# One-pass input fold, and 5 of 6 instead of 2 of 3 steps that take their mirrored values from the even part

## Chip, cores, metric

One core of a Trainium2 chip. The metric is the device time of one execution in microseconds (us). All profiled runs are fast; the granted clock of the tensor engine is 0.99 to 1.00 of full speed on the mean of every profile. Ratios are the mean time of one kernel's fast runs over the mean of the other's fast runs of the same rounds, so they differ slightly from the ratio of the medians that are quoted beside them.

## The reference

```python
def _attn_ref(x):                        # x: (8, 3008, 256)
    X = np.fft.fft(x, axis=1)
    X = np.fft.fft(X, axis=2)
    return X.real.astype(np.float32)

def _moe_ref(x, w_gate, w_val, w_out):   # x: 24064 x 256, d_ff 1536
    gate = np.maximum(x @ w_gate, 0.0)
    val = x @ w_val
    return (gate * val @ w_out).astype(np.float32)
```

A real part of a two-dimensional Fourier transform, then a gated feed-forward layer.

## The kernel before

The transform is done by matmuls. Because the input is real and only the real part is wanted, the input is first *folded*: rows s and S-s, columns d and D-d are added and subtracted, and half of the tokens are computed together with their *mirrors* (token S-s). There are 288 steps (8 batches x 3 blocks x 12 slices of d_ff). A step computes 512 tokens of 128 hidden units: gate `G` and value `V` for the tokens, and again for their mirrors. With even part `P` and odd part `Q`, the token is `P + Q` and the mirror `P - Q`. The mirror of the gate is made by a matmul that adds -2Q to `G` in PSUM (the memory that matmuls write to). The mirror of the value is made in one of two ways:

- *unsplit* step: a matmul adds -2Q to `V` ("mirrored value matmul"), and VectorE multiplies gate and value of the mirror;
- *split* step: VectorE saves the even part `E` between the two value matmuls (`even`), later computes 2E - V, and GpSimd multiplies.

```python
    ep = ctx.enter_context(tc.tile_pool(name="ep", bufs=4, space=SB))   # rings of gm and E
    ...
    def split(t):
        return NBLK * NF + 8 <= t < len(steps) and t % 3 != 2
    def mirror_gate(t): ...
        nc.tensor.matmul(e["G"][:, cols], lhsT=wm[0][...], rhs=pqt[b, blk][:, 1, cols],
                         start=False, stop=True, skip_group_check=True)
        e["gm"] = ep.tile([128, 512], F32, tag="gm", name="gm")
        nc.scalar.activation(e["gm"][:, cols], e["G"][:, cols], ACTF.Relu)
    def value(t, part): ...              # part 0: V = P;  part 1: V += Q, then h = gs * V on VectorE
    def even(t): ...                     # E = nb * af + V   (VectorE, between part 0 and part 1)
    def mirror_value(t):
        ...
        if split(t):
            nc.vector.scalar_tensor_tensor(e["E"][:, cols], e["E"][:, cols], 2.0, e["V"][:, cols],
                                           op0=ALU.mult, op1=ALU.subtract)
            mirror_h(t, nc.gpsimd, e["E"])          # h = gm * E on GpSimd
        else:
            nc.tensor.matmul(e["V"][:, cols], lhsT=wm[1][...], rhs=pqt[b, blk][:, 1, cols],
                             start=False, stop=True, skip_group_check=True)
            mirror_h(t, nc.vector, e["V"])
    ...
    for t in range(n + NF):              # one step; `extra` holds loads, transforms of the next batch
        if 0 < t <= n: mirror_gate(t - 1)
        if t < n:      gate(t)
        if 0 < t <= n: value(t - 1, 1) if split(t - 1) else mirror_value(t - 1)
        if t < n and not split(t): value(t, 0); value(t, 1)
        for fn in extra.get(t, ()): fn()
        if t >= NF: out_piece(t - NF, 0)
        if split(t): value(t, 0); even(t)
        if t >= NF: out_piece(t - NF, 1)
        if 0 < t <= n and split(t - 1): mirror_value(t - 1)
        ...                              # one operation of a running fold, on GpSimd (two early on)
```

GpSimd's stream is in program order: the operations of the fold for the batch after next stand between its products `h = gm * E`. A fold of a batch has five chunks. (`if`/`else` condensed above; the whole kernel follows.)

Of the kernel before, what the change touches and what calls it, by code (L numbers as in the profile page):

```python
# [11 lines left out]
F32 = mybir.dt.float32  # L12
BF16 = mybir.dt.bfloat16
I32 = mybir.dt.int32
ALU = mybir.AluOpType
ACTF = mybir.ActivationFunctionType
SB = bass.MemoryType.SB
# [9 lines left out]
def free(ap, offset, *dims):  # L27

    part = list(ap.ap[0])
    return bass.AP(ap.tensor, ap.offset + offset, [part] + [list(d) for d in dims])  # L30
# [12 lines left out]
def kernel(ctx: ExitStack, tc, x, w_gate, w_val, w_out, out):  # L43
# [4 lines left out]
    B, S, D = x.shape  # L48
    DF = w_gate.shape[1]
    NA, NB = 94, 32  # L50
    H = D // 2
    NF = DF // 128
    NKA = 12
    NBLK = 3
    J = NB // 2 + 1

    const = ctx.enter_context(tc.tile_pool(name="const", bufs=1, space=SB))
    xp = ctx.enter_context(tc.tile_pool(name="xp", bufs=1, space=SB))
    xcp = ctx.enter_context(tc.tile_pool(name="xcp", bufs=2, space=SB))
    tp = ctx.enter_context(tc.tile_pool(name="tp", bufs=2, space=SB))  # L60
    hp = ctx.enter_context(tc.tile_pool(name="hp", bufs=2 * NF + 1, space=SB))
    psd = ctx.enter_context(tc.tile_pool(name="psd", bufs=1, space=PS))
# [13 lines left out]
    XC = 3  # L76
# [12 lines left out]

    def fold(b, eng):  # L90

        xl, xh, eo = xt[b]
        for lo in range(1, J - 1, XC):
            hi = min(lo + XC, J - 1)
            n = hi - lo
            x1, e1 = xl[0:NA, lo:hi, :], eo[:, lo:hi, :]
            rev = free(xh[0:NA], (NB // 2 - lo) * D, [-D, n], [1, D])
            c1 = xcp.tile([NA, XC, D], F32, tag="xc", name="xc")[:, 0:n, :]
            yield eng.tensor_tensor(c1, x1, rev, op=ALU.subtract)  # L99
            yield eng.tensor_tensor(x1, x1, rev, op=ALU.add)  # L100
            yield eng.tensor_tensor(e1[:, :, H + 1:D], c1[:, :, 1:H], free(c1, D - 1, [D, n], [-1, H - 1]),
                                    op=ALU.subtract)
            eng.tensor_copy(free(e1, 0, [D, n], [H, 2]), free(x1, 0, [D, n], [H, 2]))
            yield eng.tensor_tensor(e1[:, :, 1:H], x1[:, :, 1:H], free(x1, D - 1, [D, n], [-1, H - 1]), op=ALU.add)  # L104
        ends = free(xl[0:NA], 0, [(J - 1) * D, 2], [H, 2])
        eng.tensor_copy(free(eo[:], 0, [(J - 1) * D, 2], [H, 2]), ends)
        for op, o in ((ALU.add, 1), (ALU.subtract, H + 1)):
            yield eng.tensor_tensor(
                free(eo[:], o, [(J - 1) * D, 2], [1, H - 1]), free(xl[0:NA], 1, [(J - 1) * D, 2], [1, H - 1]),
                free(xl[0:NA], D - 1, [(J - 1) * D, 2], [-1, H - 1]), op=op)  # L110
# [158 lines left out]
    with tc.tile_pool(name="sp", bufs=1, space=SB) as sp:  # L269
# [88 lines left out]
        for cs, (o0, d1) in enumerate(((8.0, -8.0), (16.0, -8.0))):  # L358
            o = sp.tile([128, 1], F32, tag=f"off{cs}")
# [13 lines left out]
        for cs in range(2):  # L373
            t2 = sp.tile([128, 4, NB], F32, tag=f"m2t{cs}")
# [27 lines left out]
        for _ in fold(1, nc.gpsimd):  # L402
            pass
# [13 lines left out]
    op = ctx.enter_context(tc.tile_pool(name="op", bufs=2, space=SB))  # L417

    steps = [(b, blk, f) for b in range(B) for blk in range(NBLK) for f in range(NF)]
# [6 lines left out]

    def split(t):

        return NBLK * NF + 8 <= t < len(steps) and t % 3 != 2

    def gate(t):
        b, blk, f = steps[t]
        pq, fs = pqt[b, blk], slice(f * 128, (f + 1) * 128)
        e = ht[t] = {"h": hp.tile([128, 2, 512], BF16, tag="h", name="h"),
                     "G": psg.tile([128, 512], F32, tag="g", name="G"),
                     "gs": gp.tile([128, 512], F32, tag="gs", name="gs")}
        nc.tensor.matmul(e["G"][:], lhsT=wc[0][:, fs], rhs=pq[:, 0, :], start=True, stop=False)  # L437
        nc.tensor.matmul(e["G"][:], lhsT=ws[0][:, fs], rhs=pq[:, 1, :], start=False, stop=True)  # L438
        nc.scalar.activation(e["gs"][:], e["G"][:], ACTF.Relu)  # L439
        cols = mirrored(t)  # L440
        if cols.stop - cols.start < 512:

            lo = 0 if cols.start else cols.stop
            nc.gpsimd.memset(e["h"][:, 1, lo:lo + NB], 0.0)

    def mirror_gate(t):
        b, blk, f = steps[t]
        e, cols = ht[t], mirrored(t)
        nc.tensor.matmul(e["G"][:, cols], lhsT=wm[0][:, f * 128:(f + 1) * 128], rhs=pqt[b, blk][:, 1, cols],  # L449
# [4 lines that stand above are left out]
    def value(t, part):  # L454
        b, blk, f = steps[t]
        e, pq, fs = ht[t], pqt[b, blk], slice(f * 128, (f + 1) * 128)
        if part == 0:
            e["V"] = psv.tile([128, 512], F32, tag="v", name="V")
            nc.tensor.matmul(e["V"][:], lhsT=wc[1][:, fs], rhs=pq[:, 0, :], start=True, stop=split(t))  # L459
        else:  # L460
            nc.tensor.matmul(e["V"][:], lhsT=ws[1][:, fs], rhs=pq[:, 1, :], start=False, stop=True,  # L461
                             skip_group_check=split(t))
            nc.vector.tensor_tensor(e["h"][:, 0, :], e["gs"][:], e["V"][:], op=ALU.mult)  # L463

    def even(t):
        b, blk, f = steps[t]
        e, cols = ht[t], mirrored(t)
        e["E"] = ep.tile([128, 512], F32, tag="e", name="E")
        nc.vector.scalar_tensor_tensor(e["E"][:, cols], nbt[b, blk][:, cols], af[:, f:f + 1], e["V"][:, cols],  # L469
                                       op0=ALU.mult, op1=ALU.add)  # L470
# [8 lines left out]
    def mirror_value(t):  # L479
        b, blk, f = steps[t]  # L480
        e, cols = ht[t], mirrored(t)
# [3 lines that stand above are left out]
            mirror_h(t, nc.gpsimd, e["E"])  # L485
        else:
            nc.tensor.matmul(e["V"][:, cols], lhsT=wm[1][:, f * 128:(f + 1) * 128], rhs=pqt[b, blk][:, 1, cols],  # L487
                             start=False, stop=True, skip_group_check=True)
            mirror_h(t, nc.vector, e["V"])
# [38 lines left out]
    def at(t, fn, *args):  # L528
        extra.setdefault(t, []).append(lambda: fn(*args))

    for k in range(4):
# [3 lines left out]
    at(9, nyquist)  # L535


    plan = {0: (28, 34, (14, 16, 18, 19, 21, 23, 24, 25), 26, 33, (33, 34, 36, 38, 40, 42)),
            1: (12, 19, range(11, 19), 19, 26, (26, 27, 29, 31, 33, 35)),
            2: (7, 13, range(6, 14), 14, 22, (23, 25, 27, 29, 31, 33))}  # L540
    for b in range(B):
        t0 = b * NBLK * NF
        tl, tf, t1, tsh, tr, t2 = plan[min(b, 2)]
        if b + 2 < B:
            at(t0 + tl, load_x, b + 2, nc.sync)
            at(t0 + tf, lambda b=b: folds.append(fold(b + 2, nc.gpsimd)))
        if b + 1 < B:
            for c, k in zip((1, 2, 3, 4, 5, 6, 7, 0), t1):
                at(t0 + k, stage1, b + 1, c, "act")
            at(t0 + tsh, shuffle_out, b + 1, 0, 8)  # L550
            at(t0 + tsh, shuffle_in, b + 1, 0, NKA)
            at(t0 + tr, rotate, b + 1)
            for i, k in enumerate(t2):
                at(t0 + k, stage2, b + 1, i // 2, i % 2, "act")

    folds = []
    n = len(steps)
    for t in range(n + NF):
        if 0 < t <= n:
            mirror_gate(t - 1)  # L560
        if t < n:
            gate(t)
        if 0 < t <= n:
            if split(t - 1):
                value(t - 1, 1)
            else:
                mirror_value(t - 1)
        if t < n and not split(t):
            value(t, 0)
            value(t, 1)  # L570
        for fn in extra.get(t, ()):
            fn()
        if t >= NF:
            out_piece(t - NF, 0)
        if split(t):
            value(t, 0)
            even(t)
        if t >= NF:
            out_piece(t - NF, 1)
        if 0 < t <= n and split(t - 1):  # L580
            mirror_value(t - 1)
        for k in range(2 if t < NBLK * NF + 8 else 1):
            while folds and next(folds[0], folds) is folds:
                folds.pop(0)


# [28 lines left out]
```

## Time and profile before

| | before |
|---|---|
| time, median of 3 (675.66 with the fourth run, used below) | 675.4 us (675.08 to 675.92) |
| PE / VectorE / ScalarE / GpSimd busy | 643.4 / 500.8 / 428.9 / 428.5 us of 673.5 |
| mirrored value matmuls | 126 |
| chain that ended last | PE 94% |

The page of the kernel before, its busy times, slices of GpSimd and PE, and its chain (DVE is VectorE, ACT is ScalarE, POOL is GpSimd):

```profile
PE 643.4 (96%) x4218; PEld 419.9 (62%) x4297; DVE 500.8 (74%) x800; ACT 428.9 (64%) x811; POOL 428.5 (64%) x590
...
PE   2899999999999999999999999999999999999996
...
POOL 1218910994999499946997399946997344344341
...
PE 94%; DMA 2%; DVE 2%; issue 1%; ACT 1%; SPq 0%; DVEq 0%; ACTq 0%
```

PE is full from about 36 us on, and GpSimd is full only in stretches: those are the folds. The groups of instructions of the same page (count, then busy us and mean ns of one, then idle time before them and what ended it):

```profile
L475 POOL TENSOR_TENSOR h<-gm,E 128x480 bf16<-128x480 f32 (+1 forms) x162 | 199.1, 1229 | 147.9 <-DVE E L483 147.2
...
L469 DVE SCALAR_TENSOR_TENSOR E<-nb,af,V 128x480 f32<-128x480 bf16 (+1 forms) x162 | 117.2, 723 | 7.4 <-PE V L459 5.9
...
L483 DVE SCALAR_TENSOR_TENSOR E<-E,V 128x480 f32<-128x480 f32 (+1 forms) x162 | 106.6, 658 | 0.0
...
L487 PE MATMUL V<-pq,wm_108 128*128 128x480 bf16 (+1 forms) x126 | 46.6, 370 | 0.2
L99 POOL TENSOR_TENSOR xc<-xl,xh 94x768 f32<-94x768 f32 x35 | 63.6, 1817 | 39.6 <-DMA xl<-in_x_dram 24.8
L100 POOL TENSOR_TENSOR xl<-xl,xh 94x768 f32<-94x768 f32 x35 | 63.5, 1814 | 1.2
```

L487 is the mirrored value matmul, L475 GpSimd's product, L469 and L483 VectorE's two operations for the mirror's value. A matmul's 370 ns is latency; what it costs PE is the distance between starts. The timeline of the kernel before, matmuls and VectorE only (start us, duration us, what):

```profile
621.52 0.38 PE L459 MATMUL V<-pq,wc_104 128*128 128x512 bf16 x1
621.54 0.69 DVE L475 TENSOR_TENSOR h<-gm,V 128x512 bf16<-128x512 f32 x1 [0.47 <-ACT gm L452]
...
622.14 0.74 DVE L469 SCALAR_TENSOR_TENSOR E<-nb,af,V 128x512 f32<-128x512 bf16 x1
...
622.39 0.38 PE L437 MATMUL G<-pq,wc_103 128*128 128x512 bf16 x1
622.61 0.38 PE L438 MATMUL G<-pq,ws_105 128*128 128x512 bf16 x1
622.94 0.38 PE L461 MATMUL V<-pq,ws_106 128*128 128x512 bf16 x1
```

L437 to L438 is 0.22 us, one slot. L438 to L461 is 0.33: a *hole* of 0.11 us. The second value matmul L461 overwrites `V`, so it must wait until VectorE has read it for `E` (L469 ends at 622.88), and VectorE first did the unsplit step's product (L475). No view of waits lists this hole, because the modelled end of the previous matmul covers it.

### The profile page before, as it was taken

The page shows a single profiled execution, that of the slowest core. Times are in us where ns is not written, and L with a number is a line of the kernel's source. Part 1 is how long each engine was busy: PE and PEld are TensorE (multiplying, and loading weights), DVE is VectorE, ACT ScalarE, POOL GpSimd, SP SyncE. Part 2 cuts the span into 40 slices and gives each one's busy share as a digit, 9 for nine tenths or more (in the row PEclk, how much of TensorE's full clock was granted, in tenths as well). Part 3 has the DMA queues.
Part 4 walks back from the last instruction along what each step waited for, and adds up shares of the span by engine and source line. Part 5 has one row for each costly group of instructions (what it writes and reads, how often), then busy time and mean ns, then how long its engine had stood idle before and what let it go on. Part 6 is the DMA issues. An engine that isn't in the chain of part 4 may idle for free.

```text
span 673.5 us, 12515 instructions
## 1 busy us (share of the span) xinstructions
PE 643.4 (96%) x4218; PEld 419.9 (62%) x4297; DVE 500.8 (74%) x800; ACT 428.9 (64%) x811; POOL 428.5 (64%) x590
## 2 busy tenths in 40 slices
PE   2899999999999999999999999999999999999996
PEld 1444665666666666666666666666666666666665
DVE  8446555567787787887888888878878788888881
ACT  5455665667566757676666767676676766656562
POOL 1218910994999499946997399946997344344341
PEclk9999999999999999999999999999999999999999
DMA  9693138229413932277112931268211231211113
GB/s 240 209 224 47 43 97 236 63 52 216 147 48 90 231 97 57 60 158 212 47 45 66 228 119 41 77 142 212 57 46 51 69 107 39 79 33 46 46 33 92
DMA packets 31844, 70.75 MB, mean 105 GB/s; under 512 B 4410, under 2 KB 21426, under 8 KB 29394
## 3 DMA queue, kind: packets, MB, share of 16 engines
q1 hardware_dynamic: 29444, 58.16, 31.9%
q0 software_dynamic: 2336, 11.80, 8.7%
q8 instruction: 33, 0.54, 0.4%
q14 instruction: 31, 0.25, 0.1%
HBM read 39.77 MB, written 30.96 MB: 105 GB/s over the span
## 4 chain that ended last, share of the span: by engine, by line
PE 94%; DMA 2%; DVE 2%; issue 1%; ACT 1%; SPq 0%; DVEq 0%; ACTq 0%
PE po L505 38%; PE G L438 10%; PE V L461 9%; PE G L449 9%; PE V L459 8%; PE G L437 8%; PE V L487 4%; PE psw L251 4%; DMA xh<-in_x_dram 2%; DVE h L463 1%; DVE eo L130 0%; DVE E L469 0%; SPq L119 0%; ACT gm L452 0%; ACT os L508 0%
## 5 line engine op out<-in xcount | busy, mean ns | idle before, releaser
L505 PE MATMUL po<-wo,h 128*128 128x256 bf16 x2304 | 323.3, 273 | 1.8
L475 POOL TENSOR_TENSOR h<-gm,E 128x480 bf16<-128x480 f32 (+1 forms) x162 | 199.1, 1229 | 147.9 <-DVE E L483 147.2
L505 PEld LDWEIGHTS <-h 128*128 128x128 bf16 x2304 | 222.8, 98 | 82.7 <-issue 7.6
L452 ACT ACTIVATE gm<-G 128x480 f32<-128x480 f32 (+1 forms) x288 | 167.4, 581 | 134.0 <-PE G L449 130.4
L463 DVE TENSOR_TENSOR h<-gs,V 128x512 bf16<-128x512 f32 x288 | 190.6, 684 | 47.5 <-PE V L461 40.4
L439 ACT ACTIVATE gs<-G 128x512 f32<-128x512 f32 x288 | 171.8, 597 | 2.2 <-POOL si L399 2.2
L475 DVE TENSOR_TENSOR h<-gm,V 128x480 bf16<-128x480 f32 (+1 forms) x126 | 83.7, 664 | 87.8 <-ACT gm L452 63.2
L469 DVE SCALAR_TENSOR_TENSOR E<-nb,af,V 128x480 f32<-128x480 bf16 (+1 forms) x162 | 117.2, 723 | 7.4 <-PE V L459 5.9
L438 PE MATMUL G<-pq,ws_105 128*128 128x512 bf16 x287 | 108.8, 379 | 2.0
L449 PE MATMUL G<-pq,wm_107 128*128 128x480 bf16 (+1 forms) x288 | 106.7, 371 | 1.0 <-ACT gs L439 1.0
L483 DVE SCALAR_TENSOR_TENSOR E<-E,V 128x480 f32<-128x480 f32 (+1 forms) x162 | 106.6, 658 | 0.0
L461 PE MATMUL V<-pq,ws_106 128*128 128x512 bf16 x272 | 103.0, 379 | 0.2
L459 PE MATMUL V<-pq,wc_104 128*128 128x512 bf16 x265 | 100.5, 379 | 0.0
L508 ACT COPY os<-po 128x512 f32<-128x512 f32 x96 | 56.2, 585 | 68.3 <-PE po L505 68.3
L437 PE MATMUL G<-pq,wc_103 128*128 128x512 bf16 x249 | 94.4, 379 | 1.0 <-ACT pq L206 1.0
L99 POOL TENSOR_TENSOR xc<-xl,xh 94x768 f32<-94x768 f32 x35 | 63.6, 1817 | 39.6 <-DMA xl<-in_x_dram 24.8
L100 POOL TENSOR_TENSOR xl<-xl,xh 94x768 f32<-94x768 f32 x35 | 63.5, 1814 | 1.2
L461 PEld LDWEIGHTS <-ws_106 128*128 128x128 bf16 x288 | 28.2, 98 | 33.8 <-DVE ws_106 L256 0.4
L438 PEld LDWEIGHTS <-ws_105 128*128 128x128 bf16 x288 | 28.2, 98 | 32.4 <-issue 1.1
L487 PE MATMUL V<-pq,wm_108 128*128 128x480 bf16 (+1 forms) x126 | 46.6, 370 | 0.2
L459 PEld LDWEIGHTS <-wc_104 128*128 128x128 bf16 x288 | 28.2, 98 | 17.5 <-issue 1.3
L104 POOL TENSOR_TENSOR eo<-xl 94x381 bf16<-94x381 f32 x35 | 34.8, 995 | 0.0
(362 smaller groups left out, 401.5 us busy)
## 6 DMA issues: line engine op xcount, KB each, us to landing
out_dram<-os SPq DMA_DIRECT2D x176, 128.0 KB
xl<-in_x_dram SPq DMA_DIRECT2D x7, 1360.0 KB
nb<-Nd SPq DMA_DIRECT2D x24, 128.0 KB
xl<-in_x_dram SPq DMA_DIRECT2D x7, 238.0 KB
xl<-in_x_dram SPq DMA_DIRECT2D x2, 768.0 KB
xh<-in_x_dram SPq DMA_DIRECT2D x2, 768.0 KB
wst<-in_moe_w_gate_dram SPq DMA_DIRECT2D x6, 256.0 KB
wst<-in_moe_w_val_dram SPq DMA_DIRECT2D x6, 256.0 KB
```

The lines of the kernel that those rows point to most:

```text
L437: nc.tensor.matmul(e["G"][:], lhsT=wc[0][:, fs], rhs=pq[:, 0, :], start=True, stop=False)
L438: nc.tensor.matmul(e["G"][:], lhsT=ws[0][:, fs], rhs=pq[:, 1, :], start=False, stop=True)
L439: nc.scalar.activation(e["gs"][:], e["G"][:], ACTF.Relu)
L449: nc.tensor.matmul(e["G"][:, cols], lhsT=wm[0][:, f * 128:(f + 1) * 128], rhs=pqt[b, blk][:, 1, cols], start=False, stop=True, skip_group_ ...
L452: nc.scalar.activation(e["gm"][:, cols], e["G"][:, cols], ACTF.Relu)
L459: nc.tensor.matmul(e["V"][:], lhsT=wc[1][:, fs], rhs=pq[:, 0, :], start=True, stop=split(t))
L461: nc.tensor.matmul(e["V"][:], lhsT=ws[1][:, fs], rhs=pq[:, 1, :], start=False, stop=True, skip_group_check=split(t))
L463: nc.vector.tensor_tensor(e["h"][:, 0, :], e["gs"][:], e["V"][:], op=ALU.mult)
L469: nc.vector.scalar_tensor_tensor(e["E"][:, cols], nbt[b, blk][:, cols], af[:, f:f + 1], e["V"][:, cols], op0=ALU.mult, op1=ALU.add)
L475: eng.tensor_tensor(free(e["h"][:], 512 + cols.start + NB - 1, [NB, (cols.stop - cols.start) // NB], [-1, NB]), e["gm"][:, cols].rearrange ...
L483: nc.vector.scalar_tensor_tensor(e["E"][:, cols], e["E"][:, cols], 2.0, e["V"][:, cols], op0=ALU.mult, op1=ALU.subtract)
L505: nc.tensor.matmul(po[:, s % 2, :], lhsT=ht[t - f + ff]["h"][:, sg, g * 128:(g + 1) * 128], rhs=wo[:, ff, :], start=(ff == 0), stop=(ff == ...
```

## The change

The intent: take 63 more mirrored value matmuls off PE (5 of 6 steps split, from step 18 instead of 44), and pay for GpSimd's additional products by a fold with one pass less. With u[d] = x[s,d] + x[S-s,D-d], the cosine part is u[d] + u[D-d] and the sine part u[d] - u[D-d]: one full pass instead of a sum and a difference. The timetable of loads, folds and transforms is moved to suit. (Stage 1, shuffle, rotation and stage 2 are the parts of the next batch's transform; only the step in which each is issued matters here.)

```diff
-    xcp = ctx.enter_context(tc.tile_pool(name="xcp", bufs=2, space=SB))
@@ def fold(b, eng), for each chunk of 3 columns
-            rev = free(xh[0:NA], (NB // 2 - lo) * D, [-D, n], [1, D])
-            c1 = xcp.tile([NA, XC, D], F32, tag="xc", name="xc")[:, 0:n, :]
-            yield eng.tensor_tensor(c1, x1, rev, op=ALU.subtract)
-            yield eng.tensor_tensor(x1, x1, rev, op=ALU.add)
-            yield eng.tensor_tensor(e1[:, :, H + 1:D], c1[:, :, 1:H], free(c1, D - 1, [D, n], [-1, H - 1]),
-                                    op=ALU.subtract)
-            eng.tensor_copy(free(e1, 0, [D, n], [H, 2]), free(x1, 0, [D, n], [H, 2]))
-            yield eng.tensor_tensor(e1[:, :, 1:H], x1[:, :, 1:H], free(x1, D - 1, [D, n], [-1, H - 1]), op=ALU.add)
+            eng.tensor_tensor(free(e1, 0, [D, n], [H, 2]), free(x1, 0, [D, n], [H, 2]),
+                              free(xh[0:NA], m, [-D, n], [H, 2]), op=ALU.add)
+            yield eng.tensor_tensor(x1[:, :, 1:D], x1[:, :, 1:D], free(xh[0:NA], m + D - 1, [-D, n], [-1, D - 1]),
+                                    op=ALU.add)
+            for op, o in ((ALU.add, 1), (ALU.subtract, H + 1)):
+                yield eng.tensor_tensor(e1[:, :, o:o + H - 1], x1[:, :, 1:H], free(x1, D - 1, [D, n], [-1, H - 1]),
+                                        op=op)
@@ def split(t)
-        return NBLK * NF + 8 <= t < len(steps) and t % 3 != 2
+        return 18 <= t < len(steps) and t % 6 != 5
@@ timetable: step of the load, of the fold's start, of stage 1, shuffle, rotation, stage 2
-    plan = {0: (28, 34, (14, 16, 18, 19, 21, 23, 24, 25), 26, 33, (33, 34, 36, 38, 40, 42)),
-            1: (12, 19, range(11, 19), 19, 26, (26, 27, 29, 31, 33, 35)),
-            2: (7, 13, range(6, 14), 14, 22, (23, 25, 27, 29, 31, 33))}
+    plan = {0: (18, 24, (16, 17, 18, 19, 20, 21, 22, 23), 24, 31, (32, 33, 35, 37, 39, 41)),
+            1: (7, 13, range(6, 14), 14, 22, (23, 25, 27, 29, 31, 33))}
@@ end of a step
-        for k in range(2 if t < NBLK * NF + 8 else 1):
-            while folds and next(folds[0], folds) is folds:
-                folds.pop(0)
+        while folds and next(folds[0], folds) is folds:
+            folds.pop(0)
```

More of the change, by code (lines that the diff above doesn't have):

```diff
@@ L93, in fold @@
         for lo in range(1, J - 1, XC):
-            hi = min(lo + XC, J - 1)
-            n = hi - lo
-            x1, e1 = xl[0:NA, lo:hi, :], eo[:, lo:hi, :]
-            rev = free(xh[0:NA], (NB // 2 - lo) * D, [-D, n], [1, D])
-            c1 = xcp.tile([NA, XC, D], F32, tag="xc", name="xc")[:, 0:n, :]
-            yield eng.tensor_tensor(c1, x1, rev, op=ALU.subtract)
-            yield eng.tensor_tensor(x1, x1, rev, op=ALU.add)
-            yield eng.tensor_tensor(e1[:, :, H + 1:D], c1[:, :, 1:H], free(c1, D - 1, [D, n], [-1, H - 1]),
-                                    op=ALU.subtract)
-            eng.tensor_copy(free(e1, 0, [D, n], [H, 2]), free(x1, 0, [D, n], [H, 2]))
-            yield eng.tensor_tensor(e1[:, :, 1:H], x1[:, :, 1:H], free(x1, D - 1, [D, n], [-1, H - 1]), op=ALU.add)
+            n = min(XC, J - 1 - lo)
+            x1, e1, m = xl[0:NA, lo:lo + n, :], eo[:, lo:lo + n, :], (NB // 2 - lo) * D
+            eng.tensor_tensor(free(e1, 0, [D, n], [H, 2]), free(x1, 0, [D, n], [H, 2]),
[5 more added lines that the diff above has]
+                                        op=op)
         ends = free(xl[0:NA], 0, [(J - 1) * D, 2], [H, 2])
@@ L535 @@
     at(9, nyquist)
-    plan = {0: (28, 34, (14, 16, 18, 19, 21, 23, 24, 25), 26, 33, (33, 34, 36, 38, 40, 42)),
-            1: (12, 19, range(11, 19), 19, 26, (26, 27, 29, 31, 33, 35)),
-            2: (7, 13, range(6, 14), 14, 22, (23, 25, 27, 29, 31, 33))}
+    plan = {0: (18, 24, (16, 17, 18, 19, 20, 21, 22, 23), 24, 31, (32, 33, 35, 37, 39, 41)),
+            1: (7, 13, range(6, 14), 14, 22, (23, 25, 27, 29, 31, 33))}
     for b in range(B):
         t0 = b * NBLK * NF
-        tl, tf, t1, tsh, tr, t2 = plan[min(b, 2)]
+        tl, tf, t1, tsh, tr, t2 = plan[min(b, 1)]
         if b + 2 < B:
```

## The prediction

> **What bounds the kernel now.** The tensor engine (PE): 643.4 us busy of 673.5 on the page, 94% of the chain that ended last. Busy PE alone proves little: the Trainium skill ("Perfetto Trace Analysis", Identifying the Most-Contended Engine) says so. The timeline settles it: matmuls start every 0.216 us (512 columns), 0.20 (480) and 0.109 (256), almost without holes, from 36 to 658 us, and the list of waits has only 1.1 us of PE after 150 us. The skill's "TensorE: Matmul & The Clock Gate" gives 215.7 ns for 512 columns; this trace agrees. The others have room: VectorE 74%, ScalarE 64%, GpSimd 64%.
>
> **What the change removes.** Split steps go from 162 to 225 of 288 (22 more in steps 18 to 43, 41 later). Each of the 63 loses its mirrored value matmul; listed at 370 ns, but that is latency, and on PE it occupies one slot. 19 slots of 0.216 and 44 of 0.203 us: **-13.0 us**, all on the critical path.
>
> **What it adds and moves.** A new split step takes 0.72 + 0.66 us (even part, mirror value) instead of a 0.66 us product on VectorE: +45 us, to about 81%. Within a run of five split steps VectorE issues 0.60 + 0.63 + 0.64 = 1.87 to 1.9 us per step against PE's 1.93: it just keeps up. GpSimd gets 63 products of 1.23 us (+77); the fold loses a 1.8 us pass per chunk: 5.8 to about 4.0 us, 35 times, -63. GpSimd ends near 440 us.
>
> **Holes in PE.** Before, the second value matmul of the first split step after an unsplit one often starts 0.11 us late: VectorE does the unsplit step's mirrored product first, so the even part, which that matmul waits for, is late. Some 80 such places become 45: about -1.5 us.
>
> **What comes back.** While a fold runs, GpSimd gets more work than PE's steps last: 17 steps bring 20.9 us of fold, 15 x 1.22 of products and some memsets, 39.8 us, against 34.7 of PE. The backlog reaches about 5 us. The E and gm rings have 4 buffers; by the distances in the timeline, a backlog of about 4 us delays ScalarE's gm and soon PE's mirrored gate matmul. Before, it peaked at 4.3 us and cost 2.9 us of ScalarE and 1 us of PE. I expect 0.5 to 1 us of PE stall in each of six folds, **+4 us**. The second batch's fold now starts at step 24 among split steps and may wait 1 to 3 us for its load (13.5 us before): +0.5. Start and tail do not change.
>
> **Prediction.** 675.4 - 13.0 - 1.5 + 3.6 = **664.5 us**, 80% range 659.5 to 669.5. Faster by over 2% (below 661.9): 0.23; within 2%: 0.75; slower by over 2%: 0.02.
>
> **What would show it.** Mirrored value matmuls 63 instead of 126, still one slot each; PE busy about 630 us, still over 92% of the chain; VectorE about 545, GpSimd about 440 us; late in each fold, mirrored products starting 4 to 5 us after their E is ready; waits of gm (ScalarE) or E (VectorE) on GpSimd's products of 5 to 15 us in all, and PE waits of a few us on gs or E there.
>
> **What would make it wrong.** If the backlog stays harmless: 660 to 661. If VectorE, at 97% within a run of five, slips behind, every second value matmul waits for E: some 0.1 us x 180 lost. If GpSimd blocks on a late load, the products behind it stall everything for several us a batch. The reversed 255-wide add could be slower than the 1.8 us pass.

## The result

The changed kernel takes 669.56 us (669.35 to 669.77, 4 runs) against 675.66 us; ratio 0.991 (0.9893 to 0.9927). The forecast was 664.5 us with 659.5 to 669.5: the direction was right, the class (within 2%) was right, and the time lies just above the range: a gain of 10.9 us was forecast, 6.1 came. The page and the chain after, and its groups:

```profile
PE 631.9 (95%) x4157; PEld 413.5 (62%) x4234; DVE 544.4 (82%) x863; ACT 429.2 (64%) x811; POOL 444.9 (67%) x618
...
PE 78%; POOL 9%; issue 5%; DVE 4%; DMA 2%; ACT 1%; SPq 0%; POOLq 0%; DVEq 0%
```

```profile
L473 POOL TENSOR_TENSOR h<-gm,E 128x480 bf16<-128x480 f32 (+1 forms) x225 | 276.1, 1227 | 154.3 <-DVE E L481 133.9
...
L485 PE MATMUL V<-pq,wm 128*128 128x480 bf16 (+1 forms) x63 | 23.3, 370 | 0.2
...
L98 POOL TENSOR_TENSOR xl<-xl,xh 94x765 f32<-94x765 f32 x35 | 63.3, 1807 | 2.7
```

63 mirrored value matmuls are gone, one of the two 1.8 us passes of the fold too, and the busy times are those forecast (PE 630, VectorE 545, GpSimd 440). What differs is the chain: GpSimd is now 9% of it and "issue" 5%. From the lists of waits between 60 and 670 us (total us, times, longest us), first before, then after:

```profile
POOL xc L99 <- DMA xh<-in_x_dram,ix: 2.2, 3, 0.9
...
ACT gm L452 <- POOL h L475: 1.0, 1, 1.0
PE G L449 <- ACT gs L439: 1.0, 1, 1.0
```

```profile
ACT gm L450 <- POOL h L473: 26.6, 32, 1.4
...
PE G L447 <- ACT gs L437: 6.5, 7, 1.0
POOL eo L96 <- DMA xh<-in_x_dram,ix: 6.4, 5, 2.2
...
DVE E L467 <- POOL h L473: 2.7, 9, 0.4
```

The first shows ScalarE's `gm` almost never waiting for a GpSimd product, the second 32 times. One such place in the timeline of the changed kernel, late in the fold that runs in the third batch (step 27 of that batch):

```profile
255.28 1.27 POOL L473 TENSOR_TENSOR h<-gm,E 128x512 bf16<-128x512 f32 x1
...
256.58 0.57 ACT L450 ACTIVATE gm<-G 128x480 f32<-128x480 f32 x1 [1.41 <-POOL h L473]
256.59 0.71 DVE L467 SCALAR_TENSOR_TENSOR E<-nb,af,V 128x480 f32<-128x480 bf16 x1 [0.38 <-POOL h L473]
257.05 0.59 ACT L437 ACTIVATE gs<-G 128x512 f32<-128x512 f32 x1
...
257.69 0.36 PE L447 MATMUL G<-pq,wm 128*128 128x480 bf16 x1 [0.97 <-ACT gs L437]
```

A GpSimd product ends late (256.55). It was the last reader of the buffer that `gm` needs, so ScalarE, idle for 1.4 us, starts `gm` only then; the next operation in ScalarE's order, `gs`, follows late; the mirrored gate matmul overwrites what `gs` reads, so PE stands still for 1 us. The E ring delays VectorE at the same moment.

To see all of it I took the start of every matmul, subtracted the start of the one before it in program order and its slot (0.2155, 0.2025, 0.1085, 0.0555 us for 512, 480, 256, 128 columns), and called what is left a hole. This needs no modelled ends. (79 matmul records are missing from the profile before and 77 from that after, against 4297 and 4234 weight loads; a missing one is counted with its slot.) Holes over 0.04 us between 68 and 650 us, summed, by the matmul that came late. "Lag" is the time from the end of 2E - V to the start of the product on GpSimd, the peak over the third to sixth batch. (The wait of 1.0 us for `gs` in the list before stands at 61 us, outside this window; the changed kernel has the same one at 62.6 us.)

| kernel | time, us | mirrored gate | second value | other | sum | peak lag |
|---|---|---|---|---|---|---|
| before | 675.66 | 0.0 | 4.6 | 2.9 | 7.5 | 4.5 |
| after | 669.56 | 7.0 | 6.3 | 0.3 | 13.5 | 6.5 |
| after, again | 670.20 | 8.4 | 6.8 | 0.0 | 15.3 | 6.5 |

So the removed slots were nearly half spent again on holes: with the small ones the sum is 9.7 us before and 15.7 after. -13.0 us of slots + 6.0 of holes + 1.4 of a later opening (see below) is -5.5; the two profiles differ by -5.9 us.

### The profile page after: what moved, and what is told of

Read it like the earlier page. It is cut to its first block, busy times and chain, and to the rows that moved or that the text cites. A ratio compares the mean times of both kernels' runs of the same rounds, so it can differ in the third digit from the quotient of the medians.

```text
span 667.6 us, 12589 instructions
## 1 busy us (share of the span) xinstructions
PE 631.9 (95%) x4157; PEld 413.5 (62%) x4234; DVE 544.4 (82%) x863; ACT 429.2 (64%) x811; POOL 444.9 (67%) x618
## 4 chain that ended last, share of the span: by engine, by line
PE 78%; POOL 9%; issue 5%; DVE 4%; DMA 2%; ACT 1%; SPq 0%; POOLq 0%; DVEq 0%
PE po L503 33%; PE V L459 9%; PE G L436 9%; PE G L447 8%; PE V L457 7%; PE G L435 7%; POOL h L473 4%; POOL eo L101 3%; DMA xh<-in_x_dram 2%; POOL xl L98 2%; PE psw L249 2%; PE V L485 2%; PE ps L159 2%; DVE E L467 1%; PE ps L201 1%
## 5 line engine op out<-in xcount | busy, mean ns | idle before, releaser
L473 POOL TENSOR_TENSOR h<-gm,E 128x480 bf16<-128x480 f32 (+1 forms) x225 | 276.1, 1227 | 154.3 <-DVE E L481 133.9
L467 DVE SCALAR_TENSOR_TENSOR E<-nb,af,V 128x480 f32<-128x480 bf16 (+1 forms) x225 | 162.9, 724 | 15.6 <-PE V L457 9.1
L447 PE MATMUL G<-pq,wm 128*128 128x480 bf16 (+1 forms) x288 | 106.6, 370 | 7.5 <-ACT gs L437 7.5
L436 PE MATMUL G<-pq,ws 128*128 128x512 bf16 x283 | 107.2, 379 | 2.3
L459 PE MATMUL V<-pq,ws 128*128 128x512 bf16 x284 | 107.5, 378 | 1.7 <-DVE E L467 0.8
L457 PE MATMUL V<-pq,wc 128*128 128x512 bf16 x263 | 99.7, 379 | 0.0
L435 PE MATMUL G<-pq,wc 128*128 128x512 bf16 x245 | 92.8, 379 | 1.0 <-ACT pq L204 1.0
L98 POOL TENSOR_TENSOR xl<-xl,xh 94x765 f32<-94x765 f32 x35 | 63.3, 1807 | 2.7
L459 PEld LDWEIGHTS <-ws 128*128 128x128 bf16 x288 | 28.1, 98 | 34.1 <-DVE ws L254 0.4
L436 PEld LDWEIGHTS <-ws 128*128 128x128 bf16 x288 | 28.1, 98 | 32.5 <-issue 1.1
L435 PEld LDWEIGHTS <-wc 128*128 128x128 bf16 x288 | 28.1, 98 | 15.1 <-issue 11.5
L457 PEld LDWEIGHTS <-wc 128*128 128x128 bf16 x288 | 28.1, 98 | 13.1 <-issue 4.8
```

What stands on the lines that cost most here:

```text
L435: nc.tensor.matmul(e["G"][:], lhsT=wc[0][:, fs], rhs=pq[:, 0, :], start=True, stop=False)
L436: nc.tensor.matmul(e["G"][:], lhsT=ws[0][:, fs], rhs=pq[:, 1, :], start=False, stop=True)
L447: nc.tensor.matmul(e["G"][:, cols], lhsT=wm[0][:, f * 128:(f + 1) * 128], rhs=pqt[b, blk][:, 1, cols], start=False, stop=True, skip_group_ ...
L457: nc.tensor.matmul(e["V"][:], lhsT=wc[1][:, fs], rhs=pq[:, 0, :], start=True, stop=split(t))
L459: nc.tensor.matmul(e["V"][:], lhsT=ws[1][:, fs], rhs=pq[:, 1, :], start=False, stop=True, skip_group_check=split(t))
L467: nc.vector.scalar_tensor_tensor(e["E"][:, cols], nbt[b, blk][:, cols], af[:, f:f + 1], e["V"][:, cols], op0=ALU.mult, op1=ALU.add)
```

## The experiments

Theory A: in a fold, GpSimd gets more work than PE's steps last; its backlog reaches PE through the 4-buffer rings of `gm` and `E`. Rival B: VectorE, with 1.87 to 1.9 us of work per split step of 1.93 us, slows PE, and GpSimd only looks late. Inside A: A1, the loads that the folds wait for are the missing part; A2, the fold's own work was underestimated.

### Both rings with 6 buffers

```diff
-    ep = ctx.enter_context(tc.tile_pool(name="ep", bufs=4, space=SB))
+    ep = ctx.enter_context(tc.tile_pool(name="ep", bufs=6, space=SB))
```

> The changed kernel with 6 instead of 4 buffers for both E and gm; nothing else. Theory A (the GpSimd backlog in the folds reaches PE through the rings: gm late, gs late, mirrored gate matmul late): the late mirrored gate matmuls (7.2 us of holes between 68 and 650 us) and the late second value matmuls at steps 4 of each six (2.3 us) vanish, time about 660.5 us, ratio to before 0.978. Rival B (VectorE at 97% in a run of five is what slows PE, GpSimd only looks late): the rings do nothing, 669 to 670 us.

Measured: 658.66 us (before 675.84), ratio 0.9744 (0.9728 to 0.976), clearly faster than before. Holes 3.35 us: mirrored gate 0.0, second value 3.25 (2.9 of it after unsplit steps). The peak lag grew to 7.8 us and harmed nothing; so the 6.5 us of the changed kernel is a backlog that the rings of 4 held down. The list of waits of rings6 (60 to 670 us):

```profile
POOL eo L96 <- DMA xh<-in_x_dram,ix: 8.3, 5, 2.8
...
ACT gm L450 <- POOL h L473: 2.3, 3, 1.0
...
PE G L447 <- ACT gs L437: 1.0, 1, 1.0
```

`gm` waits 2.3 us for GpSimd's products instead of 26.6. The same VectorE work is done, so rival B falls. This run also checks the size of the removed slots: spans 656.3 and 673.5 differ by 17.2 us, all holes changed by -4.0 (9.7 to 5.6), and -13.0 - 4.0 is -17.0.

### Only gm, only E

(The comments name the run; they are not in the code.)

```diff
-        e["gm"] = ep.tile([128, 512], F32, tag="gm", name="gm")                 # gm6
+        e["gm"] = ep.tile([128, 512], F32, tag="gm", bufs=6, name="gm")
-        e["E"] = ep.tile([128, 512], F32, tag="e", name="E")                    # e6
+        e["E"] = ep.tile([128, 512], F32, tag="e", bufs=6, name="E")
```

> Only gm gets 6 buffers, E stays at 4. Theory A with gm as the ring that matters: mirrored gate holes go from 7.2 to under 1 us, the late second value matmuls (E) stay at 2 to 4 us, as VectorE now waits where ScalarE did before; time about 663 us. If E is the tighter ring, the time stays above 667 us. Rival B: 669 to 670 us.

> Only E gets 6 buffers, gm stays at 4. Theory A: only the 2.3 us of late second value matmuls at steps 4 of six go, the mirrored gate holes stay at about 7 us; time 667 to 668.5 us. If E is the tighter ring: about 663 us. Rival B: 669 to 670 us.

Measured: 669.13 us (0.9896, 0.9879 to 0.9912) with gm alone and 668.74 us (0.9888, 0.9871 to 0.9904) with E alone: neither helps. From the list of waits of gm6 (60 to 670 us), then of e6:

```profile
PE V L459 <- DVE E L467: 7.7, 11, 1.1
...
ACT gm L450 <- POOL h L473: 0.9, 1, 0.9
```

```profile
ACT gm L450 <- POOL h L473: 29.3, 40, 1.6
...
PE G L447 <- ACT gs L437: 7.2, 9, 1.2
```

With a deeper gm ring the holes go to the second value matmul (13.7 us, mirrored gate 0.0); with a deeper E ring they go to the mirrored gate (9.8 us, second value 4.2). The sum is 14.0 us both times. My expectation for gm6 (663 us) was wrong, and e6 is just above its 667 to 668.5 us, with more mirrored gate holes than the 7 us that I expected to stay: the rings are equally tight, and only lengthening both helps.

### Loads four steps earlier

```diff
-            1: (7, 13, range(6, 14), 14, 22, (23, 25, 27, 29, 31, 33))}
+            1: (3, 13, range(6, 14), 14, 22, (23, 25, 27, 29, 31, 33))}
```

> The loads for the third batch after the first and later are issued 4 steps earlier (step 3 of the batch instead of 7), the folds stay where they are. Theory A1 (my backlog was underestimated because the first fold operation waits 1 to 2 us for its load and holds the products behind it): the wait of the fold's first operation on the load (6.4 us in all) goes to nearly 0, the peak lag of the mirrored products falls from 6.5 to about 5 us, the mirrored gate holes from 7.2 to 1 to 3 us, time about 664.5 us. Theory A2 (the fold itself is more work than I summed; the load wait only fills idle time): peak lag stays above 6 us and the time within 1 us of 669.5.

Measured: 667.23 us (0.9866, 0.9848 to 0.9884), less gain than expected. The lag did fall to 5.1 to 5.5 us, but a new wait came once, here in the timeline of this kernel:

```profile
154.32 0.59 ACT L506 COPY os<-po 128x512 f32<-128x512 f32 x1 [4.67 <-DMA out_dram<-os]
...
155.94 0.58 PE L447 MATMUL G<-pq,wm 128*128 128x512 bf16 x1 [3.79 <-ACT gs L437]
...
156.33 0.63 PE L435 MATMUL G<-pq,wc 128*128 128x512 bf16 x1
...
156.75 0.63 PE L436 MATMUL G<-pq,ws 128*128 128x512 bf16 x1
```

ScalarE waited 4.7 us for a store of the output to free its buffer, and PE 3.8 us for ScalarE. The stall cost more than its length: the granted clock was half from 154.5 to 161.4 us, the starts of 512-column matmuls lie about 0.42 us apart there instead of 0.22, and by the holes this took another 2.7 us. (In the other profiles but old_fold the longest hole from 68 to 650 us is 2.6 us, and the clock stays full.) The timeline of the queue that issues transfers in order (SPq) shows why the store was late:

```profile
136.16 0.78 SPq L81 DMA_DIRECT2D xl<-in_x_dram  x2
137.44 0.23 SPq L210 DMA_DIRECT2D Nd<-pq  x1
149.40 0.35 SPq L211 DMA_DIRECT2D nb<-Nd  x1
149.85 1.77 SPq L515 DMA_DIRECT2D out_dram<-os  x4
```

L210 writes 1 KB that L211 reads back. Issued just after the 1.6 MB load, the 1 KB took 11.6 us to land (the longest wait of L211 on it), and the stores of the output stood behind L211. Only in the second batch does a load at step 3 come before such a write, as the first batch's timetable has its last stage 2 five steps into the next batch. So I left that batch alone:

```diff
+            2: (3, 13, range(6, 14), 14, 22, (23, 25, 27, 29, 31, 33))}     # from the third batch on (comment added)
...
+        tl, tf, t1, tsh, tr, t2 = plan[min(b, 2)]
```

> As load_early, but the load of the second batch's step 3 goes back to step 7, as there the queue that issues loads and stores in order was held by the load and a store of the output came 4.7 us late for ScalarE. From the third batch on loads stay at step 3. Theory A1 (late loads are the part of the backlog that I missed): three or four folds lose 0.3 to 0.6 us instead of 1.4, no 4 us hole, time 664 to 666 us. Theory A2: within 1 us of 669.

Measured: 664.12 us (0.9823, 0.9802 to 0.9844); no such wait. The backlog's holes (without those after unsplit steps) by batch in which the fold runs:

| batch | 2nd | 3rd | 4th | 5th | 6th |
|---|---|---|---|---|---|
| after | 2.8 | 1.8 | 2.1 | 1.5 | 1.6 |
| after, again | 3.4 | 2.1 | 2.1 | 1.6 | 2.3 |
| load_early2 (2nd batch as in after) | 3.5 | 0.5 | 0.9 | 0.5 | 0.8 |

The lag in the four changed batches is 5.5 us instead of 6.5. In these four folds A1 holds for the greater part: the late load is 0.8 to 1.6 us of the 1.5 to 2.3 us per fold. What is left, 0.5 to 0.9 us, agrees with the "0.5 to 1 us" of the prediction. For the second batch's fold, the dearest, this is not shown: its load was left where it was, and in load_early the stall hides it. The timelines show the wait at the first operation of a fold, here of the fold that runs in the third batch, before and after:

```profile
235.20 1.81 POOL L99 TENSOR_TENSOR xc<-xl,xh 94x768 f32<-94x768 f32 x1 [0.68 <-DMA xh<-in_x_dram,ix]
```

```profile
231.43 0.22 POOL L96 TENSOR_TENSOR eo<-xl,xh 94x6 bf16<-94x6 f32 x1 [1.28 <-DMA xh<-in_x_dram,ix]
231.73 1.81 POOL L98 TENSOR_TENSOR xl<-xl,xh 94x765 f32<-94x765 f32 x1
233.49 1.29 POOL L473 TENSOR_TENSOR h<-gm,E 128x512 bf16<-128x512 f32 x1
```

While GpSimd waits, the products that stand behind the fold's operation in its stream wait too.

### The fold in 2 of 3 steps

```diff
+        if t < NBLK * NF or t % 3 != 1:
             while folds and next(folds[0], folds) is folds:
                 folds.pop(0)
```

> The changed kernel with 4 buffers, but from the second batch on a fold operation goes out in only 2 of 3 steps, so that a fold lasts 25 instead of 17 steps; same work, same loads, same start. Theory A: GpSimd has 2.0 us per step and gets at most about 1.9, the peak lag falls to 2.5 to 4 us and the mirrored gate holes to under 1 us, time 659 to 661 us. If instead the late loads alone cause the loss, the first fold operation still waits 6 to 8 us in all and the time stays over 666 us.

Measured: 659.38 us (0.9757, 0.9736 to 0.9777). The lag is 1.7 us, no late mirrored gate matmul, holes 4.1 us. Same work, same 4 buffers: the loss was one of timing. One thing is mixed in: step 13 of a batch is a skipped one, so folds start a step later, and all waits for loads but one of 2.3 us vanish as well. How much of the gain is the missing waits and how much the slower pace is not separated here. That the waits alone are not all of it is shown by load_early2: without them 0.5 to 0.9 us per fold remain in the third to sixth batch (2.8 together), and spread has 1.0 in the same four. And rings6, with 8.3 us of the same waits, has almost no such holes.

### The old fold under the new split, and the new fold alone

`old_fold` is the changed kernel with the two-pass fold; `new_fold_only` is the kernel before with the one-pass fold (both edits are the fold's lines of the diff above, and the pool `xcp`).

> The changed kernel, 5 of 6 steps split and the new timetable, but with the old fold of two passes (5.8 instead of about 4.0 us per chunk). Theory A (GpSimd work in the fold decides): a chunk now brings 4 steps of products and 5.8 us, about 10 us against 8 us of PE, so each fold overruns the slack by 5 us or more; six folds lose 25 to 40 us, the late mirrored gate matmuls sum to over 30 us, and the time is 685 to 700 us, worse than before the change. Rival B (VectorE is what slows PE): about 670 us, as now.

> The kernel before with only the fold replaced: 2 of 3 steps split, old timetable. Theory A: GpSimd falls from 428 to about 365 us busy, its peak lag from 4.3 to 2 to 3 us, but PE lost almost nothing to it before, so the time stays at 674 to 676 us. The single fold is worth nothing by itself, it only makes room.

Measured: old_fold 698.61 us (1.0333, 1.0308 to 1.0358), 44 us of holes (mirrored gate 14.0, second value 27.6); GpSimd 503.1 us busy. The wait moved more to E than I had said (I expected over 30 us before mirrored gate matmuls); without the 2.9 us after unsplit steps the sum is 41 us, just above the 25 to 40 expected. Some 2.8 us of it are again slots at half clock, from 168.9 to 175.7 us: the clock fell in a stall of PE of 3.4 us (166.6 to 170.0). new_fold_only 675.24 us (0.9994, 0.9969 to 1.0019), GpSimd 370.1 us busy, lag at most 3.4 us. The cheaper fold is worth nothing alone, but 29 us (698.61 to 669.56) under the new split. It is what the change stands on.

### Repeat, both remedies, and all steps split

`after_again` is the changed kernel unaltered. `spread_rings6` has both remedies. `all_rings6` and `all_spread_rings6` also split every step:

```diff
-        return 18 <= t < len(steps) and t % 6 != 5
+        return 18 <= t < len(steps)
```

> The changed kernel unaltered, for a second profile. Its first profile began the steps 1.4 us later than that of before, while the five other kernels with the same opening began them at 36.4 to 37.6 us. If that was chance in the landing of the weights, this profile begins them at 36.2 to 38.4 us, and the holes between 68 and 650 us repeat: 15.7 us, of which 7.0 before mirrored gate matmuls and 6.3 before second value matmuls. Time 669 to 670 us.

> The spread fold and 6 buffers for E and gm together. Each alone already takes away the backlog's holes, so together they give nothing more: 658 to 660 us, holes 5 to 6 us, all but 1 us of them before the second value matmul after an unsplit step.

> All steps from 18 on split, 6 buffers, fold in every step. 45 more mirrored value matmuls go (-9.3 us), and with them the 3 us of late second value matmuls after unsplit steps. GpSimd gets 3 x 1.23 of products and 4 us of fold per 3 steps of 1.93: 1.9 us too much per chunk, peak lag 8 to 11 us against a slack of about 8: holes of 1 to 2 us per fold, 648 to 655 us. Rival B (VectorE is the limit: 1.89 us per step now with no unsplit step to catch up in): second value matmuls late everywhere, 660 us or more.

> All steps from 18 on split, 6 buffers, fold in 2 of 3 steps. Theory A: GpSimd 1.23 + 0.9 us per step of 1.93, a lag that grows by about 0.1 to 0.2 us per step over 25 steps, 3 to 6 us, within the slack; 646 to 650 us, holes under 3 us. Rival B: 660 us or more, with second value matmuls late in every step.

| kernel | time, us | ratio (95%) | mirrored gate holes | second value holes | other | steps begin at |
|---|---|---|---|---|---|---|
| after_again | 670.20 | 0.9912 (0.9895 to 0.9928) | 8.4 | 6.8 | 0.0 | 36.8 |
| spread_rings6 | 659.02 | 0.9739 (0.9723 to 0.9755) | 0.0 | 3.2 | 0.4 | 38.5 |
| all_rings6 | 662.49 | 0.9808 (0.9784 to 0.9832) | 0.0 | 15.4 | 0.3 | 37.6 |
| all_spread_rings6 | 652.45 | 0.9637 (0.962 to 0.9654) | 0.0 | 4.5 | 1.6 | 37.7 |

The repeat settles the opening: the first step (its first `gs` on ScalarE) begins at 36.2 to 38.5 us in all these kernels, whose openings are the same except for the fold; 38.35 in the first profile of the changed kernel was chance (before: 36.92). The sum of the holes, 15.3 against 13.5 us, repeats only roughly. Both remedies together give no more than one, as expected. all_rings6 came out worse than expected (662.49 against 648 to 655; whether it is 2% faster than before is unclear): GpSimd's lag reaches 10.8 us and 6 buffers are too few; 8.2 us of its holes lie in the second batch, which still carries the previous fold. With the fold spread as well, every step split, 652.45 us is the fastest kernel, 3.6% below before, 2.5 us above the top of what I expected, with 6.1 us of holes instead of under 3. VectorE is 89% busy there and PE has only 4.5 us of holes before second value matmuls: rival B falls a second time.

## Why the prediction was right or wrong

- **PE is the bound; the removed matmul costs a slot (0.2 us), not its listed 370 ns. Right.** -13.0 us; rings6 closes to within 0.2 us with it.
- **Added and moved work. Right.** VectorE 545 forecast, 544.4 measured; GpSimd 440 and 444.9; PE 630 and 631.9. VectorE keeps up.
- **Holes after unsplit steps. Right in kind, a little too large:** -1.5 forecast; 4.6 us before, 3.6 after (3.8 in the repeat).
- **"What comes back", the backlog. Right in mechanism, place and path (gm, gs, mirrored gate matmul, late in the folds), wrong in size. This is the step that failed.** Forecast: a backlog of 5 us, 0.5 to 1 us of stall per fold, +4 us. Measured: a lag of 6.5 us, 1.5 to 2.8 us per fold in five folds, and none in the first, 9.7 us in all (11.5 in the repeat). The term that was too small is the wait of the fold's first operation for its load. I had counted it for one fold alone (+0.5), the one that starts at step 24 of the first batch, and that one did not wait; the kernel before already showed 0.5 to 0.9 us of it in each of the later folds, which cost nothing there. After, it is 6.4 us over the five other folds (8.4 in the repeat), and with the loads earlier the remaining loss is 0.5 to 0.9 us per fold in the four folds tried, as forecast. The waits of gm and E on GpSimd's products are 29.3 us, not 5 to 15. The "chain still over 92% PE" failed with it: it is 78%. One of the numbers that the estimate leaned on was misread: the 1 us of PE that the backlog is said to have cost before stands at 61 us, where ScalarE was late because it waited 2.1 us for VectorE's conversion of weights. In the folds of the kernel before, the backlog cost PE nothing (mirrored gate holes 0.0).
- **A slip in the sum.** The text has +4 and +0.5 of losses but the sum takes 3.6. With 4.5 it would have read 665.4 us, and the range would have moved with it; that would have been nearer by luck alone, with the backlog still mis-sized.
- **Not foreseen, in favour:** before has 2.9 us of holes where stage 2 follows the rotation in the same step (twice, in the first two batches). The new timetable puts stage 2 one step later there, and no such hole is left. new_fold_only keeps the old timetable and its 2.9 us. **Not foreseen, by chance:** the opening, +1.4 us in the first profile and -0.2 in the second.

Together, for the repeat: -13.0 of slots, all holes 9.7 to 17.5 (+7.8), opening -0.2: -5.4 us; the profiles differ by 5.5 (668.0 and 673.5).

Why the load is later in relation to the fold than before, the timelines tell in part. In the second batch the new timetable itself did it: load to fold is 6 steps (7 to 13) instead of 7 (12 to 19). GpSimd was free for the fold 14.2 us after the load of `xh` was issued, instead of 16.8, and the load took 16.3 us (16.8 before): a wait of 2.2 us instead of 0.03. In the fourth to sixth batch the lead is six steps in both kernels: GpSimd was free after 17.8 us (before 18.0), and the load took 18.7 us on the mean, in the repeat 19.0 (before 18.6). So of the longer wait (1.0 us on the mean, in the repeat 1.3, before 0.7) the shorter steps are 0.2 us, and the rest is a later landing.

What stays open: why the load lands later there (or whether it is scatter), and what the new timetable alone is worth; no run has the new split with the old timetable.

## What to carry to other kernels

Work that is moved to a slack engine must fit not only the average but every stretch: compare the work per step with the step's length over the length of the burst, add the waits at the burst's head, and hold the peak lag against the buffers between that engine and the critical one. If rings of equal depth run side by side, it may be all of them or none: here one alone helped nothing. Or better spread the burst, which cost no memory here and did the same. When the critical engine gets faster, look again at every load that is timed in steps. And a long stall can cost more than its length: twice here the clock fell to half for 6.8 us in a stall of PE, of 3.4 and 3.8 us, which took some 2.7 us more.

## What the Trainium skill lacked or had wrong

- "TensorE: Matmul & The Clock Gate", Back-to-back issue gap: it calls N/2.4 + 2.5 ns the isolated gap and gives 131 ns (512 columns) and 81 ns (128 columns) for a sustained stream of weight loads and matmuls. Here, with a weight load before every matmul, the median distance of starts after a 512-column matmul is 216 ns over the whole steady part, and 56 ns at 128 columns in groups of four: the "isolated" formula holds in the stream.
- "Perfetto Trace Analysis", Optimization Strategy: it says that consistent bubbles can mean too few buffers. That was so (holes of up to 1.1 us once per fold), but the page does not say that two rings can be tight together: 6 buffers for one of them left 14.0 us of holes, for both 3.35.
- The same page, Identifying the Most-Contended Engine, warns of busy PE. It could add that waits of PE below about 0.16 us do not show as idle time at all, as the modelled end of a 512-column matmul (0.38 us) covers them: before, all 4.6 us of holes before second value matmuls were absent from the list of PE's waits.
- "DMA: Bandwidth & Descriptors", Queues, rings and completion order, says that each DMA engine consumes the descriptors of a ring in order, but not what that costs a small transfer. Here a 1 KB write issued behind a 1.6 MB load took 11.6 us to land; the issuing queue, waiting for it, held the stores, and a store's buffer came 4.7 us late.
